# A fused attention and GLU kernel: first batch's loads re-paced, the chain of replicated rows moved, stores two blocks behind

## The chip, the cores and the metric

The kernel runs on one core of a Trainium2 chip. The metric is the device time of one execution in microseconds (us). Every time of a kernel below is a median of several executions, unless it is called a single run; every reading of a profile comes from one profiled execution of that kernel. The profile of the kernel before that the prediction read is of a run of 715.1 us, longer than all its timed runs at that time and marked as slow; a second profile of it, of an ordinary run, was taken among the experiments, and the trace kept with that run is of a third, shorter execution. The accounts below give all three, since they differ.

In the timed sets the runs marked slow are those over 1.5% above the fastest of their kernel in the set; the ratios below leave them out, the medians and ranges contain them.

## The reference

Two stages run one after the other. The input x has 4 batches of 12416 tokens with 128 channels.

```python
def mab(q, kv):
    s = scale * (q @ kv.transpose(0, 2, 1))
    a = np.exp(s - s.max(-1, keepdims=True))
    a /= a.sum(-1, keepdims=True) + 1e-09
    return a @ kv
h = mab(I, x)            # 32 inducing points attend to the tokens
y = mab(x, h)            # the tokens attend to the 32 results
gate = 1 / (1 + np.exp(-(y @ w_gate)))      # w_gate, w_val: 128 x 1536
out = (gate * (y @ w_val)) @ w_out          # w_out: 1536 x 128
```

## The kernel before

A block is 512 tokens; a batch has 24 blocks. For every block TensorE, ScalarE and VectorE work as a pipeline: TensorE makes six pairs of gate chunks `g` and twelve value chunks (`va` two at a time, `vb` one), ScalarE takes tanh of each `g` into `T`, and VectorE makes `u = (T + 1) * v`, one instruction for each `va` or `vb`, whereupon TensorE adds up the output `acc`. VectorE needs about 7 us for a block (666.2 us of busy time over 97 blocks in the profile below). In six blocks of 24 (3, 7, 11, 15, 19, 23: the "shared" blocks) three of the twelve value chunks are multiplied by GpSimd instead.

A string, PLAN, fixes the interleaving of these steps. Everything else is hung into that order: `at(n, k, f)` emits `f` at step `k` (0 to 3) of block `n` (a shared block is short: what stands at its step 0 is emitted with step 1), `put` queues a job for TensorE. Each engine and each queue is given its work in exactly the order emitted. Two side chains matter here.

The chain of replicated rows makes, for every 4096 tokens, the normalised weights that the GLU blocks read (`rep`). Eight blocks use one `rep`. `n` is a block about six before the first use:

```python
def rep_events(n, b, d):
    put(n, 1, "s2", b, d)              # TensorE scores, ScalarE exp
    at(n + 1, 0, e2_dma, b, d)         # transpose e2 -> e2n       (sync queue)
    at(n + 1, 3, s2_sum, b, d)         # row sums rs, a tree of 5  (GpSimd)
    at(n + 2, 3, s2_rec, b, d)         # rc = 1 / rs               (VectorE)
    at(n + 2, 3, a2_mul, b, d, 0)      # a = e2n * rc              (GpSimd)
    at(n + 2, 3, a2_mul, b, d, 1)
    at(n + 3, 0, a2_dma, b, d, 0)      # transpose a -> a2T        (sync queue)
    at(n + 3, 1, a2_dma, b, d, 1)
    at(n + 3, 2, rep_put, b, d, 0)     # a2T -> DRAM tile dt       (sync queue)
    at(n + 3, 3, rep_put, b, d, 1)
    at(n + 4, 0, rep_get, b, d, 0)     # dt -> rep, 4 copies       (sync queue)
    at(n + 4, 1, rep_get, b, d, 1)
```

The chain of the next batch loads x in six quarters of 512 KB (`xq`, issued on GpSimd's queue), transposes each (`xT`, sync queue) and computes the scores `s_1` and sums `h` for it between the GLU steps. Finished output blocks are transposed (`on`, sync queue) and stored (GpSimd's queue), one block after they are done:

```python
loads = ((1, 0), (2, 0), (5, 0), (6, 0), (8, 0), (9, 0))     # first batch
at(n0 + ln + 1, 2, xT_dma, nb, q)
# ... (cut)
if stores and (done_out[n] == 10 or n >= NBK - 2):
    stores.popleft()()
```

The softmax here doesn't subtract the row's maximum and nothing guards it: scores larger than these inputs give would overflow.

## Time and profile before

| | before |
|---|---|
| median (3 runs) | 709.57 us (707.03 to 714.02) |
| profiled run (slow) | 715.09 us |
| profiled span | 713.3 us |
| VectorE busy | 666.2 us |
| VectorE idle, 40 to 700 us | 20.2 us |

The head of the page of the kernel before: busy time by engine, then the span in 40 slices of 17.8 us, a digit for each (9 is 90% busy or more; PEclk is the clock granted to TensorE, in tenths).

```profile
span 713.3 us, 13070 instructions
PE 679.8 (95%) x4561; PEld 238.2 (33%) x4561; DVE 666.2 (93%) x792; ACT 662.5 (93%) x773; POOL 309.6 (43%) x389
...
DVE  2599686999999999999999999999999999999997
PEclk9999898999999999999999999999999999999999
```

VectorE, ScalarE and TensorE are all near full except at the start and in slices 5 to 7. So idle time of VectorE is the account to keep. Its longest waits in the steady part are these (engine, tile and line, what it waited for; total us, times, longest):

```profile
DVE u_8_1670 L495 <- PE vb_2_1668 L428: 6.4, 1, 6.4
DVE u_4_1402 L495 <- PE va_1_1399 L428: 4.2, 1, 4.2
```

TensorE's own waits name the cause, the first for scores on quarters 2 and 3, the second for rep:

```profile
PE s_1_1657 L767 <- DMA xT_154<-xq_2_1174: 4.2, 1, 4.2
PE g_0_1394 L428 <- DMA rep_1_1278<-dt_1_0_1230: 3.6, 2, 2.4
```

With the slow clock after each gap (0.50 from 85 to 90 us, 0.52 from 110 to 115), the first (80 to 95 us, rep_1) cost 6.4 us of VectorE's time and the second (104 to 121 us, xT of quarter 3) 7.8 us. The transfers between 60 and 130 us (last number: us from issue to landing):

```profile
xq_2_1174<-in_x_dram POOLq DMA_DIRECT2D x1, 512.0 KB, 8.6
xq_3_1283<-in_x_dram POOLq DMA_DIRECT2D x1, 512.0 KB, 10.8
...
a2T_1_0_1172<-a_0_1_0_1147 SPq DMA_TRANSPOSE x1, 4.0
a2T_1_1_1204<-a_0_1_1_1149 SPq DMA_TRANSPOSE x1, 8.0
```

The same a2T transpose of 128 KB takes 4.0 or 8.0 us. The second, issued at 72.2 us, had two 512 KB loads beside it, issued at 67.3 and 68.4; the first, issued at 66.4, met them only towards its end.

These are a reciprocal of the row sums on VectorE and, below it, the sums on GpSimd, in the kernel before (start, duration, engine, line, operation):

```profile
188.49 0.68 DVE L495 SCALAR_TENSOR_TENSOR u_8_2828<-T_4_2773,vb_2_2826 128x512 f16<-128x512 f16 x1
189.09 0.35 DVE L361 RECIPROCAL rc_0_2835<-rs_0_2734 128x32 f32<-128x32 f32 x1
```

```profile
182.20 1.26 POOL L511 TENSOR_TENSOR x_2_2626<-vt_2_2627,v_19_1_2624 128x512 f16<-128x512 f32 x1
...
185.41 1.14 POOL L353 TENSOR_TENSOR tree_1_0_2735<-e2n_0_2682 128x512 f32<-128x512 f16 x1 [1.40 <-DMA e2n_0_2682<-e_1_0_2679]
...
188.33 0.24 POOL L353 TENSOR_TENSOR rs_0_2734<-tree_1_0_2741 128x32 f32<-128x32 f32 x1
```

The sums come after the last product `x` of the shared block, end at 188.57, and the reciprocal starts at 189.09 with nothing to wait for. It has 0.5 us to spare. (These lines do not depend on the slow run's gaps; the ordinary run's eleven reciprocals wait 1.2 us in all.)

### The profile page before, as it was taken

To read this page: it belongs to the slowest core of one execution; us is meant where nothing else is said; L and a number is where in the kernel's file an instruction comes from. 1 tells how busy PE (TensorE), PEld (TensorE's weight loads), DVE (VectorE), ACT (ScalarE), POOL (GpSimd) and SP (SyncE) were. 2 spreads that over 40 slices of the span, in tenths; PEclk is the share of its full clock that TensorE was granted. 3 is DMA by queue.
4 is the path that set the end of the run, shared out by engine and by line. 5 is a ranking of instruction groups with operands and counts; after the bars stand their busy time and mean duration, and the time that the engine had idled before them with its cause. 6 is when DMAs were issued, how large, how long until landed. Compare 5 with 4: busy or idle time off the path is not lost.

```text
span 713.3 us, 13070 instructions
## 1 busy us (share of the span) xinstructions
PE 679.8 (95%) x4561; PEld 238.2 (33%) x4561; DVE 666.2 (93%) x792; ACT 662.5 (93%) x773; POOL 309.6 (43%) x389
## 2 busy tenths in 40 slices
PE   7899788999999999999999999999999999999997
PEld 4433222333333323333333333333333333333334
DVE  2599686999999999999999999999999999999997
ACT  4699776999999999999999999999999999999995
POOL 5234504452643541743541651634723534633423
PEclk9999898999999999999999999999999999999999
DMA  9599999884888792397688584454192353263222
GB/s 177 95 110 158 183 71 187 139 184 84 145 188 130 125 209 60 90 183 135 106 187 148 111 164 103 94 142 77 39 169 67 60 149 80 60 150 74 60 53 75
DMA packets 163955, 85.95 MB, mean 120 GB/s; under 512 B 133392, under 2 KB 148144, under 8 KB 163888
## 3 DMA queue, kind: packets, MB, share of 16 engines
q1 hardware_dynamic: 143904, 45.95, 38.2%
q0 software_dynamic: 19696, 39.03, 27.1%
q8 instruction: 35, 0.57, 0.4%
q14 instruction: 32, 0.26, 0.2%
q10 hardware_dynamic: 288, 0.13, 0.1%
HBM read 39.34 MB, written 28.31 MB: 95 GB/s over the span
## 4 chain that ended last, share of the span: by engine, by line
PE 64%; ACT 10%; DVE 9%; DMA 8%; issue 4%; POOL 3%; SPq 1%; DVEq 0%; ACTq 0%; POOLq 0%
DMA xq_4_132<-in_x_dram 2%; DMA xT_154<-xq_3_1283 2%; DMA a2T_1_1_1204<-a_0_1_1_1149 1%; SPq L397 1%; DMA a1n_2_3819<-e_2_2_3703 1%; DMA on_7763<-oT_7761 1%; DMA a1n_2_6256<-e_3_2_6162 1%; DMA on_5277<-oT_5275 1%; PE acc_1687 L538 1%; DMA rep_1_1278<-dt_1_0_1230 0%; PE acc_4267 L538 0%; PE acc_2641 L538 0%; PE acc_1770 L538 0%; PE acc_5765 L538 0%; PE acc_3334 L538 0%
## 5 line engine op out<-in xcount | busy, mean ns | idle before, releaser
L538 PEld LDWEIGHTS <-wo_117 128*128 128x128 f16 x1152 | 94.2, 98 | 147.7 <-issue 93.8
L428 PEld LDWEIGHTS <-hw_165 32*128 32x128 f16 x466 | 19.1, 91 | 59.9 <-issue 54.5
L428 PEld LDWEIGHTS <-hw_168 32*128 32x128 f16 x456 | 19.8, 91 | 56.2 <-issue 53.9
L428 PEld LDWEIGHTS <-hw_167 32*128 32x128 f16 x464 | 19.4, 91 | 54.1 <-issue 51.2
L428 PEld LDWEIGHTS <-hw_166 32*128 32x128 f16 x468 | 19.4, 91 | 52.4 <-issue 49.8
L428 PEld LDWEIGHTS <-hwp_172 128*128 128x128 f16 x120 | 11.7, 97 | 14.3 <-issue 4.7
L428 PEld LDWEIGHTS <-hwp_169 128*128 128x128 f16 x110 | 10.7, 98 | 15.8 <-issue 8.6
L428 PEld LDWEIGHTS <-hwp_171 128*128 128x128 f16 x112 | 10.9, 97 | 13.7 <-issue 5.8
L428 PEld LDWEIGHTS <-hwp_170 128*128 128x128 f16 x108 | 10.5, 97 | 14.6 <-issue 7.3
L566 POOL DMA_DIRECT2D out_dram<-on_1411 x1 | 0.5, 532 | 21.3 <-DMA on_1411<-oT_1409 21.3
L245 PEld LDWEIGHTS <-ones 128*128 128x128 f16 x96 | 6.9, 97 | 8.1 <-DMA a1n_2_6256<-e_3_2_6162 2.1
L190 PE MATMUL warm<-ones 128*128 128x512 f16 x16 | 5.6, 530 | 1.5 <-DVE ones L140 1.5
L767 PE MATMUL s_1_1657<-xT_154,indT 128*32 128x512 f16 x8 | 1.2, 605 | 5.8 <-DMA xT_154<-xq_2_1174 4.2
L495 DVE SCALAR_TENSOR_TENSOR u_8_1670<-T_4_1559,vb_2_1668 128x512 f16<-128x512 f16 x1 | 0.7, 690 | 6.4 <-PE vb_2_1668 L428 6.4
L214 ACT ACTIVATE e_1_2_1666<-s_1_1657 128x1024 f16<-128x1024 f32 x1 | 1.0, 1024 | 5.9 <-PE s_1_1657 L767 5.9
L310 POOL COPY hwp_169<-hw_165 32x128 f16<-32x128 f16 x2 | 0.6, 282 | 12.9 <-ACT hw_165 L303 12.8
L239 ACT ACTIVATE a1nt_205<-s1t_203 128x32 f16<-128x32 f32 x1 | 0.2, 198 | 6.0 <-PE s1t_203 L235 6.0
L495 DVE SCALAR_TENSOR_TENSOR u_4_1402<-T_2_1358,va_1_1399 128x1024 f16<-128x1024 f16 x1 | 1.2, 1222 | 4.2 <-PE va_1_1399 L428 4.2
L566 POOL DMA_DIRECT2D out_dram<-on_888 x1 | 0.5, 537 | 10.5 <-DMA on_888<-oT_886 10.5
L508 POOL TENSOR_TENSOR vt_0_6656<-v_59_2_6653,T_0_6643 128x512 f32<-128x512 f32 x1 | 1.1, 1150 | 8.3 <-PE s_2_6670 L324 8.3
L551 ACT ACTIVATE o_10374<-acc_10278 128x256 f32<-128x256 f32 x2 | 0.8, 384 | 4.3 <-PE acc_10278 L528 3.8
L482 ACT ACTIVATE T_0_1397<-g_0_1394 128x1024 f16<-128x1024 f32 x1 | 1.0, 1024 | 3.9 <-PE va_1_1399 L428 3.9
(4281 smaller groups left out, 2802.5 us busy)
## 6 DMA issues: line engine op xcount, KB each, us to landing
xq_0_120<-in_x_dram POOLq DMA_DIRECT2D x1, 512.0 KB, 5.1
xq_1_122<-in_x_dram POOLq DMA_DIRECT2D x1, 512.0 KB, 6.9
xq_2_128<-in_x_dram POOLq DMA_DIRECT2D x1, 512.0 KB, 8.3
xq_3_130<-in_x_dram POOLq DMA_DIRECT2D x1, 512.0 KB, 10.2
xq_4_132<-in_x_dram POOLq DMA_DIRECT2D x1, 512.0 KB, 13.4
xq_5_134<-in_x_dram POOLq DMA_DIRECT2D x2, 256.0 KB, 14.1
xq_0_770<-in_x_dram POOLq DMA_DIRECT2D x1, 512.0 KB, 6.2
xq_1_875<-in_x_dram POOLq DMA_DIRECT2D x1, 512.0 KB, 10.1
```

Source lines behind the costliest of these rows:

```text
L190: nc.tensor.matmul(ps[:, 0:TOK], ones[:, 0:P], ones[:], start=True, stop=True)
L214: nc.scalar.activation(out=e1[:, 0:w], in_=ps[:, 0:w], func=AF.Exp, scale=SCALE)
L245: nc.tensor.matmul(ps[:, cs:cs + P], ones[:, 0:P], a1n[(b, q)][:, j, :], start=first and j == 0, stop=last and j == 3,)
L397: nc.sync.dma_start(rep[g * M:(g + 1) * M, 4 * i:4 * i + 4].rearrange("m r j t -> m r (j t)"), dt[:].rearrange("(r m) t -> m r t", m=M),)
L428: nc.tensor.matmul(ps[:, ds(col, TOK)], weights(k["b"]), rep[rows, 4 * k["i"] + k["r"]], start=True, stop=True,)
L482: nc.scalar.activation(out=Ts[(bi, p)][:, :, 0:T], in_=ps[:].rearrange("p (a t) -> p a t", a=2)[:, :, 0:T], func=AF.Tanh, scale=0.5,)
L495: nc.vector.scalar_tensor_tensor(out=u[:, :, 0:T], in0=Ts[(bi, j0 // 2)][:, j0 % 2:j0 % 2 + n, 0:T], scalar=1.0, in1=ps[:].rearrange("p (a ...
L508: nc.gpsimd.tensor_tensor(out=t[:], in0=v, in1=Ts[(bi, j0 // 2)][:, j0 % 2 + jj, :], op=ALU.mult)
L538: nc.tensor.matmul(accs[bi][:, 0:T], wo16[:, j, :], u, start=(c == 0), stop=(c == NJ - 1))
L551: nc.scalar.activation(out=o32[:, h:h + w, :].rearrange("p b c -> p (b c)"), in_=accs[bi][:, ds(h * P, w * P)], func=AF.Copy, scale=0.5,)
L566: nc.gpsimd.dma_start(out[ds(row0, QT)].rearrange("(p j) c -> p j c", j=QT // P)[:, 4 * k["r"]:4 * k["r"] + 4, :], on[:],)
L767: nc.tensor.matmul(ps[r * M:(r + 1) * M, ts(i, TOK)], indT[:], xTs[a[0]][:, ds(q * QT + r * TOK, TOK)], start=True, stop=True,)
```

## The change

The intent is to remove the two early gaps: the loads of the first batch come one at a time, the big transposes stand apart from the fetches of rep, these are half a block later, and stores wait another half block, so that GpSimd isn't held by an output transpose (21.3 us at one in the profile read). With this, row sums and reciprocal move one step earlier inside their blocks, and most chains also move one block earlier (`rep_events` at 1 and 9 instead of 2 and 10, and `fin` at 15 instead of 16 in the first batch).

```diff
     def rep_events(n, b, d):
         put(n, 1, "s2", b, d)
         at(n + 1, 0, e2_dma, b, d)
-        at(n + 1, 3, s2_sum, b, d)
-        at(n + 2, 3, s2_rec, b, d)
-        at(n + 2, 3, a2_mul, b, d, 0)
-        at(n + 2, 3, a2_mul, b, d, 1)
-        at(n + 3, 0, a2_dma, b, d, 0)
-        ... (cut)
+        at(n + 1, 2, s2_sum, b, d)
+        at(n + 2, 2, s2_rec, b, d)
+        for i in range(2):
+            at(n + 2, 2, a2_mul, b, d, i)
+            at(n + 3, 0, a2_dma, b, d, i)
+            at(n + 3, 3, rep_put, b, d, i)
+            at(n + 4, 2, rep_get, b, d, i)
... (cut)
-        rep_events(n0 + 2, b, 1)
-        rep_events(n0 + 10, b, 2)
+        rep_events(n0 + (2 if b == 0 else 1), b, 1)
+        rep_events(n0 + 9, b, 2)
... (cut)
-                loads = ((1, 0), (2, 0), (5, 0), (6, 0), (8, 0), (9, 0))
-                s1s, s1t, fin = (5, 9, 12), 6, 16
+                loads = ((0, 3), (2, 2), (4, 1), (6, 0), (7, 3), (9, 2))
+                s1s, s1t, fin = ((5, 1), (9, 0), (12, 1)), 6, 15
+                wait = 4                        # 6 in the later batches
... (cut)
-                at(n0 + ln + 1, 2, xT_dma, nb, q)
+                at(n0 + ln + (lk + wait) // 4, (lk + wait) % 4, xT_dma, nb, q)
... (cut)
-        if stores and (done_out[n] == 10 or n >= NBK - 2):
+        while stores and (n >= NBK - 2 or len(stores) > 1 and done_out[n] == 4):
```

The string PLAN is replaced too (the interleaving of 97 blocks), and the h jobs move a little.

More of the change, by code (lines that the diff above doesn't have):

```diff
@@ L26 @@
     "GAGBWGAabGBcGAfeGBdGAhBWgJ AGilkjBGGAabcBGAfGBedGAhGgBiG AlkjBGGAbacBGAfWBedGAhJBgG "
-    "AilkjBGGAabcBGAfWBedGAhGgBiG AlkjBGGAbaBcWAGfeBGdAGBhGg AGilkBjGAJBabcAGefBGdAGhgBGi "
-    "AGlBkjJAGBaGbAGcGBefGAdhGBgG AikljBGGAbBaefGAdGBchG AgGBikGAljBJAGaBGbcGAGfBedG "
-    "AhGgBiGAlJBkGAjJBGAGbacBfeG AGdhBgiAGlkjBGGAbBJaAGcfBGe AGdhBGgAGiBkljGAGBabef "
-    "AGdBJcGAhgBGikAGljJBGAGbaBcfG AGedBGgAGhBilGAGkjBJAGBaGbcG AefGBdGAhgGBiGAkljBJAGbaGBcf "
-    "AGeGdBhGAgiWBlGAkjJBG AGabfBecGAGdBghGAikGBlJjAGBaGbcG AfGBedGAhJBgGAilkjBGGAabBcefG "
@@ L32 @@
-    "AdGBghGAilkjBGGAbaBGcGAfBJe AGdhBGgAGilBkjGAGBabef AGdcBGgGAhiBkljGAGBbacfAGedgGBhG "
-    "AilkjBGGAbacBWAGfBedGAhGgBiG AlkjBGGAbacBJAGfBGeAGdghBG AGilBkjGAGBbafeAGdcGBG "
-    "AghBGiAGklBJjAGGBbacfAGedBGg AGhiBGkAGljBJAGBGabcGAeGfBdG AgGhBiGAlGkBjGAJbaBcAGfeBGdh "
-    "AGgiGBkGAljBJAGbGBGa AGBefdGAGchBgGAiGBlkjGAGBabce AGfBJdAGhgBWiAGkBljGAGBbacf "
-    "AGedGBghAGilkjBGGAabBGcAGefBGd AGhgBGiAGlkjBJGABbGafG AedGBcGAhgBWiGAklBjJGAaGbBcG "
-    "AfeGBdGAhJBgGAilkjBGGAbacBfe AGdgGBhGAilkjBGGAaBJbAGceBGf AGdhBGgAGilkBjGAGBabef "
@@ L38 @@
-    "AGdcGBgGAhiBGkAGljBJAGBGbaceG AGfBdghGAiWBklGAjJBGAGabcBfG AGedBhGAgGBGAGilkJjBGAaGbBGcf "
-    "AGedBWhAGgilBkjGAJaBbG AceGBfGAdhBWgGAilBkjGAJbBaG AcfGBeGAdBWghAGilkBjGGAabBceG "
-    "AfGdBgGAhiBGGAlkjBGGAbacGBe AGfdBhGAGgilBkjAGGBbafe AGcdBGhAGgiBlkjGAGBabceAGfdBgG "
-    "AGhikBljGAGBabcGAefBGdAGhgBGi AGlBkjGAGaBbcGAJBfeGAdGBhgG AilkjBGGAabfBedGAcGBhgG "
-    "AikljBJGAbGBacGAfWBedAGhgGBiG AlkGBGAjBJAGbBGacGAfGBedG AhGgBiGAlGkBjGAGBbacfAGeBJd "
-    "AGghBGiAGlkjBJGABbaGfG AedBchGGAgiBkljGAGBabceGAfBdGgh AGikljBGAJBbaGAcWBfeGAdGhBgG "
@@ L44 @@
-    "AilkjBGAGabBcGAeGBGAGfdBGh AGgikBGAGlBjJAGBbGae AGfdBGhGAgciBGAGlkBjJGABbGacG "
-    "AfGeBdGAhgWBiGAkljBJAGbacBfG AeGBdGAhJBgGAilkjBGGAbacBfGG AedBghiGAlkjBGGAbaBfedG "
-    "AGhBgciAGlkBjJGAaBbGcfAGedWBhgG AiGlBkGAjJBGAGabBcWAGfBedG AGhgBiGAlGkBjJAGBbaGGcAGfBJe "
-    "AGdBGhgGAilkBjGAGbBafeG AdcGBgGAhiGBkGAljBJGAbacBfG AeGBdhGAgGiBlGAkjBWGAabBcefG "
-    "AdGBghGAilkjBGGAbacBfeGAGBdGh AGgilBkjGAGBefbaAGdgBWh AGicBkljGAGBbacGAefdBGAGghBiG "
-    "AGlkjBGAGBbacGAfeBWdAGhgBGi AGlBkjGAGBabcGAefGBdGAhGBgiG AkljBGGAfeBbadGAhWBgcG "
@@ L50 @@
-    "AilkBjGGAabBcGAfeGBdGAhgBGiG AlkBjGGAbaBcAGfWBedGAhgGBiG AlkjBJAGbacBGAfGeBGAdWBhgG "
-    "AikljBGGAfedBabGAGhBgiG AclkjBGGAabcBGAGfBedGAhWgBiG AGlkBjGAGBbacAGefBWAGdhgBG "
-    "AGiBlkjGAGBabcAGefBdJAGGhBgG AikGlBjGAGBabfeAGdgBWh AGciBkljGAGBabcGAefBGdAGhgiBG "
-    "AGkljBGAGBbacGAfeBWdGAhgBGi AGlBkjGAGBabcGAefGBdGAJBhgG AilkjBGGAfeBbadGAGhgBcG "
-    "AilBkjGGAabBcGAfBGedGAhgWiBG AlkjBGGAbacBGAGfeBdGAGBhgiG AlkjBGGAabcBGAGfeBdGAGBGhg "
-    "AGiBlkjGAGBefabAGdhBWgG AicBlkjGAGBbacGAefBGdAGhgBGi AGlkBjGAGBbacGAefBWdGAhgBGi "
@@ L56 @@
-    "AGlBkjGAGBbacGAefGBdGAhGgBiG AlkjBGGAfebBadGAgWBhcG AikBljGGAabBcGAfeGBdGAhGBgiG "
-    "AlkBjGGAbBacAGfBWedAGhgBGiG AlkBjGAGbaBcGAefBGdGAhGgBiG AlkjBGGAbafBeGAdWBhgG "
-    "AcikBljGABaGbAcfeBdAhgBilkj"
+    "AilkjBGGAabcBGAfWBedGAhGgBiG AlkjBGGAbaBcWfAGeBGdAGhBgG AGilBkjAGJBbaAGcfBGeAGdgBGh "
+    "AGiBGlAGkBJjAGGBabceAGfdBGgG AhiBGkAGljBJAGbGBaJ AGcBGefGAdgWBhGAilkjBGGAbacBeG "
+    "AfJBdGAghWBiGAlkjBJAGabcBfeG AdGhBgGAilkjBGGAabBcGGAefBdJ AGhBGgiGAlkGBjJAGBGbafG "
+    "AedBGcGAhBJgGAiklBjGAGaBbcf AGedGBgGAhikBljGAGBbacfAGedBGhG AgiBGlAGkjBJGABbGaGAGceBJ "
@@ new lines @@
+    "AGBfGdgGAhiGBlJkjAGBGabfG AedBGcGAgBJhAGilkjBGGAbBacfG AeGdBhGAgJBiGAlkjBWGAabcBfG "
+    "AGedBhGAgGiBlGAkGjBGAGBabcf AGedBGhgGAikljBGGAbaBfeG AGdgBhGAiGBlkGAjcBWGAabcBfG "
+    "AGeBdhGAgGiBlGAkjBGGAabBceG AGfdBgGAJBhiGAlGkBjGAGBabcf AGedBGhgAGilkjBGGAabfBeG "
+    "AdGBchGAgGiBlGAkJBjGGAbacBeG AfGdBhGAgJBiGAlkjBJGAaBGbcG AeGfBdGAhgGBiGAlGkBjAGGBbacfG "
+    "AedhBgGGAilkjBJGABGbafG AedGBhGAgiGBkGAljBcWGAaBbcfG AeGdBgGAhJBiGAlkjBWGAabcBefG "
+    "AGdhBgGAilkjBGGAabBcfeGAGdBGhg AGiBkljGGAfBebaGAdgWBhG AicGBkGAljJBGAGabBcJAGfGBedG "
@@ new lines @@
+    "AhBJgAGilkBjGAJbBaGAcfWBeG AdhGBgGAikljBGAGabcBeGAfdGBGhg AGilkjBGGAfeBdGbAGahBWg "
+    "AGiklBGAGjBcJAGBGabcGAfeGBdG AhgiBGGAklBjJGABbWacGAfeGBdG AhgGBiAGlkJjBGAbGaGBcGAfGeBdG "
+    "AhGgBiGAlkjBWGAbafBJ AGBeGcAGdBhgGAGiBlkjAGJbBa AGcfBGeAGdBgGhAGilkBjGAGBabcf "
+    "AGedBGhAGgBGikAGljBGGAabBGc AGeBfGdAGhgBWAGilBkjG AGBbaefAGdhgBGAGickBljGAGBabce "
+    "AGfdBGhAGgikBljGAGBabceAGfdGBg AGhiBGlAGkBjJAGaBbcGAGfeBdG AhGgBiGAlkjBGGAbaeBfdG "
+    "AGchBgGAilkjBJGAaGBbcGAfeGBdG AhgBGiGAlBJkAGjBJAGBGbacG AfGBedGAhgGBiGAkljBGGAbaBGc "
@@ new lines @@
+    "AGfeBdhgGAGilkjBJAGBWabf AGedGBgGAhiGBlGAkjcBWAGabBceG AfdGBgGAhJBiGAlkBjWGAabBcfG "
+    "AeGdBhGAgGiBlGAkGBjGAGBabcf AGedBGhgAGilkjBGGAbaeBfG AdGhBgGAcGBilGAkjBJAGabGcBJG "
+    "ABJefGAdgGhBiGAlkjBWGAabcBJ AGfeBdGAGhBgGAiGBlkjAGGBbacG AfGeBdGAhgGBilGAkjBWG "
+    "AfebBadGAGhBgikGAljcBJGAbBWacG AfeGBdGAghBGiGAlkjBJAGbBGacG AfeGBdGAhgiBGJlkjAGBbacGGAfBJe "
+    "AGdgGBhGAilBkjGAGbaBefG AdcGBgGAhiGBlGAkjBJGAbBacfG AeGdBgGAhGBikGAljBGGAabBceG "
+    "AfGdBGAhGBgiGAlGkBjGAGBabcG AefGBdGAhGBgiGAlkBjWG AfeaBbdGAhgGBiGAlkjcBGGAbacBfG "
@@ new lines @@
+    "AeGBdgGAhGiBlGAkjBWGAbaBceG AGfBdgGAhiGBlGAkGBjGAGBabcf AGedBGhAGgikBljGAGBbaef "
+    "AGdhGBgAGciBGkAGljBWAGBabcf AGeBGdgGAhiGBlGAkjBJAGabBceG AfGdBgGAhiGBlGAkjBGGAabBcfG "
+    "AGeBdghGAilGkBjGAGBefb AGadBGgAGhiBGAGlkBjcGAGBabce AGfdhBGAGgiBlkjGAGBabcfAGedGBh "
+    "AGgiBGkAGlBJjAGGBbacAGeBfGd AGhgBGikGAljBGGAbaeBfG AdGcBhGAgGiBlGAkjBWGAbaBceG "
+    "AGfBdgGAJBhiGAlkjBWAGabcBfG AGBedhGAgGiBGAlGBkjGAGBabcf AGedBGhgGAikljBGGAbafBedG "
+    "AGgBhiGAklBjcAGGaBbcfGAedGBgG AhilBkjGAGBbacAGfeBWdAGhgBGi AGlBkjGAGBabcGAefGBdGAhgGBiG "
@@ L59 @@
+    "AlkjBGGAfeBbadGAgWBhiG AckBljGGAbBacGAfeGBdGAhgGBiG AlkBjGGAbaBcGAfWBedGAhgBGiG "
+    "AlkjBGAGbBacGAeGBfdGAGhBgi AGlkjBGGAbaBfedAGhWBgiG AclBkjGGAabBcGAfeGBdGAhgBGiG "
+    "AlkjBGGAbBacGAfWBedGAhgiBGG AlkjBGAGBbacGAefBGdGAhGBgiG AlkjBGGAfeBbaGAdWBhgG "
+    "AicBlkjGAGBabcAfedBAghBilkj"
 )
@@ L693, in rep_events @@
         at(n + 1, 0, e2_dma, b, d)
-        at(n + 1, 3, s2_sum, b, d)
-        at(n + 2, 3, s2_rec, b, d)
-        at(n + 2, 3, a2_mul, b, d, 0)
-        at(n + 2, 3, a2_mul, b, d, 1)
-        at(n + 3, 0, a2_dma, b, d, 0)
-        at(n + 3, 1, a2_dma, b, d, 1)
-        at(n + 3, 2, rep_put, b, d, 0)
-        at(n + 3, 3, rep_put, b, d, 1)
-        at(n + 4, 0, rep_get, b, d, 0)
-        at(n + 4, 1, rep_get, b, d, 1)
+        at(n + 1, 2, s2_sum, b, d)
[5 more added lines that the diff above has]
+            at(n + 4, 2, rep_get, b, d, i)
     def m_mul():
@@ L734 @@
             if b == 0:
-                loads = ((1, 0), (2, 0), (5, 0), (6, 0), (8, 0), (9, 0))
-                s1s, s1t, fin = (5, 9, 12), 6, 16
-                hs = ((8, 1), (9, 1), (12, 2), (13, 1), (14, 3), (15, 1))
+                loads = ((0, 3), (2, 2), (4, 1), (6, 0), (7, 3), (9, 2))
+                s1s, s1t, fin = ((5, 1), (9, 0), (12, 1)), 6, 15
+                hs = ((7, 1), (7, 3), (11, 1), (11, 3), (14, 1), (14, 3))
+                wait = 4
             else:
                 loads = ((-10, 0), (-7, 0), (-4, 0), (-1, 0), (2, 0), (5, 0))
-                s1s, s1t, fin = (-2, 5, 9), 0, 14
-                hs = ((1, 1), (3, 1), (7, 1), (8, 1), (12, 1), (13, 1))
+                s1s, s1t, fin = ((-2, 1), (5, 1), (9, 1)), 0, 14
+                hs = ((1, 1), (3, 1), (8, 1), (8, 3), (12, 1), (13, 1))
+                wait = 6
             for q, ((ln, lk), (hn, hk)) in enumerate(zip(loads, hs)):
                 at(n0 + ln, lk, load_x, nb, q)
-                at(n0 + ln + 1, 2, xT_dma, nb, q)
+                at(n0 + ln + (lk + wait) // 4, (lk + wait) % 4, xT_dma, nb, q)
                 put(n0 + hn, hk, "h", nb, q)
             at(n0 + loads[1][0], 1, load_tail, nb)
-            at(n0 + loads[1][0] + 1, 3, xTt_dma, nb)
-            for e, sn in enumerate(s1s):
-                put(n0 + sn, 1, "s1", nb, [2 * e, 2 * e + 1])
-                at(n0 + sn + 1, 1, a1_dma, nb, [2 * e, 2 * e + 1])
+            at(n0 + loads[1][0] + 2, 1, xTt_dma, nb)
+            for e, (sn, sk) in enumerate(s1s):
+                put(n0 + sn, sk, "s1", nb, [2 * e, 2 * e + 1])
+                at(n0 + sn + 1, 0, a1_dma, nb, [2 * e, 2 * e + 1])
             put(n0 + s1t, 1, "s1t", nb)
```

## The prediction

> **What bounds the kernel now.** In the busy time by stretch, VectorE is busy 639.8 of the 660 us between 40 and 700 us, TensorE 638.6, ScalarE 632.7: a three-engine pipeline with little to take away. What can be gained are VectorE's 20.2 us of idle time there:
>
> - 80 to 95 us: 6.4 us. The timeline shows block 8's g_0 reach TensorE at 80.6 and wait for the replicated rows rep_1 until 84.7. Their a2T_1_1 transpose took 8.0 us from 72.2, beside two 512 KB loads issued at 67.3 and 68.4.
> - 104 to 121 us: 7.8 us. The score job s_1 waits to 110.6 for the transpose xT of quarter 3, issued at 97.4, after 5.8 us of issuing quarter 2's and 4.2 us for an output transpose.
> - near 265, 365, 425 and 533 us: about 4 us. The chain of waits shows two waits for a1n transposes, and two where GpSimd waits on an output transpose before a store and delivers products late.
>
> After the first two stalls the granted clock is 0.5 for about 5 us. [...] (0.50 at 85 to 90 us), and the 1.5 us stalls leave it at 1.00.
>
> **What the change does.** Only order moves. The first batch's loads stand apart instead of in pairs; both a2T transposes follow each other at the start of block 5; stores come half a block (3.5 us) later, so GpSimd should not sit 21.3 us on one output transpose (at 88 us) with a load behind it.
>
> **Stall 2 should nearly vanish.** Quarter 3's transpose is now ahead of two output transposes, at about 84 us instead of 97, needed at about 97: 6.5 us of 7.8. **The late small ones** lose 3 of 4 us: output transposes get 3.5 us more before a store waits, and the h jobs stand further from their a1n.
>
> **Stall 1 mostly stays.** Quarter 2's transpose now stands between the a2T transposes and the dt copies. Nothing on GpSimd holds quarter 3's load back: it goes out near 67 us, not at its nominal 74, and collides with that transpose, which then takes 8 us or more, not the 4.3 us of an undisturbed one. The sync queue then issues block 5's output transpose (ready about 77) before the rep fetches; with 3.6 us to land, rep_1 arrives at 82 to 86, while g_0 of block 8 wants it at 80.6. I expect 4.5 us lost instead of 6.4.
>
> **Sum.** 6.5 + 3 + 2 = 11.5 us less in the profiled run (713.3 us, a long one). The median run's stalls must be smaller, so I take about 11 off 709.6: **698.5 us**, range 691 to 706 (removing all 20 us would give about 691). Chances: faster by over 2% 0.35, within 2% 0.61, slower 0.04.
>
> **What would show it.** VectorE idle between 104 and 121 us under 2 us, no wait of s_1 for xT; g_0 of block 8 waits 1.5 to 5 us for rep_1 near 80 us[...]; no GpSimd wait over 10 us at a store; VectorE busy still about 666 us.
>
> **What would make it wrong.** If quarter 2's transpose is quick, both stalls go: 692 to 694. If it is slow, stall 1 grows. The new interleaving could cost tenths per block, which I could not see.

## The result

The changed kernel takes 749.2 us (median of 4 runs, 748.77 to 750.69) against 708.38 for the kernel before (4 runs). The ratio is 1.056 (95% interval 1.050 to 1.063). Ratios are the mean time of one kernel's fast runs over that of the other's in the same rounds, so not quite the ratio of the medians.

The head of the page of the changed kernel, to be set against that of the kernel before:

```profile
span 747.0 us, 13067 instructions
PE 691.9 (93%) x4561; PEld 237.8 (32%) x4561; DVE 668.0 (89%) x792; ACT 664.1 (89%) x773; POOL 308.2 (41%) x389
...
DVE  2699478899799799999999799799999799899997
PEclk9999889999899999999999999899999999999999
```

VectorE is as busy as before (668.0 us against 666.2), but there are dips all along the span: besides slices 5 to 8 at 11, 14, 23, 29, 32 and 35. The kernel before has no such row of dips. Its waits (same columns as before):

```profile
DVE u_4_1402 L495 <- PE va_1_1399 L428: 12.8, 1, 12.8
DVE rc_2_1867 L361 <- POOL rs_2_1771 L353: 4.0, 1, 4.0
...
DVE rc_2_6774 L361 <- POOL rs_2_6688 L353: 3.4, 1, 3.4
DVE rc_1_5940 L361 <- POOL rs_1_5858 L353: 3.2, 1, 3.2
DVE rc_1_8323 L361 <- POOL rs_1_8242 L353: 3.1, 1, 3.1
DVE rc_1_3505 L361 <- POOL rs_1_3418 L353: 3.0, 1, 3.0
DVE rc_0_2716 L361 <- POOL rs_0_2628 L353: 3.0, 1, 3.0
DVE rc_2_9082 L361 <- POOL rs_2_8995 L353: 3.0, 1, 3.0
```

There are two kinds. One is the wait near 80 us, now 12.8 us. The other is new: seven times the reciprocal `rc` waits 3 to 4 us for GpSimd's row sums `rs`, 22.7 us in all (an eighth, in the first batch, waits 1.3 us; three of the eleven do not wait). The surroundings of one of them, on VectorE and then on GpSimd, for the same chain as those shown of the kernel before:

```profile
187.53 0.68 DVE L495 SCALAR_TENSOR_TENSOR u_3_2702<-T_1_2626,vb_1_2700 128x512 f16<-128x512 f16 x1
191.18 0.35 DVE L361 RECIPROCAL rc_0_2716<-rs_0_2628 128x32 f32<-128x32 f32 x1 [2.96 <-POOL rs_0_2628 L353]
191.44 1.16 DVE L495 SCALAR_TENSOR_TENSOR u_6_2725<-T_3_2675,va_2_2722 128x1024 f16<-128x1024 f16 x1
```

```profile
182.95 1.15 POOL L508 TENSOR_TENSOR vt_0_2611<-v_19_2_2608,T_0_2597 128x512 f32<-128x512 f32 x1 [7.91 <-ACT v_19_2_2608 L832]
...
187.98 1.15 POOL L353 TENSOR_TENSOR tree_1_0_2629<-e2n_0_2575 128x512 f32<-128x512 f16 x1
...
190.90 0.24 POOL L353 TENSOR_TENSOR rs_0_2628<-tree_1_0_2635 128x32 f32<-128x32 f32 x1
```

The reciprocal now starts when the sums end. Ahead of the sums stand the two products of the shared block, from 182.95 to 188.0. And u_6, which stands behind the reciprocal, has its value chunk from matmuls that TensorE began at 187.84 (va_2 in its timeline, 0.39 us each) and its T from ScalarE by 186.6, but it began only at 191.44: it wasn't waiting for its data but for its turn. TensorE ran dry in the meantime. Its busy time in single microseconds (stretch, length, busy us and matmuls, granted clock, DMA share, GB/s):

```profile
189.00:190.00 1.00, 0.95 (x6) 1.00 0.00 0
190.00:191.00 1.00, 0.00 (x0) 1.00 0.04 8
...
192.00:193.00 1.00, 0.34 (x2) 0.50 0.02 3
...
```

The clock stays at 0.50 until 198 us. So this wait of 2.96 us was followed by some six at half clock; around the other six waits the clock stood at 0.50 too, for two to six whole microseconds, and the 22.7 us of waiting became 32.5 us of idle VectorE. By stretches, from the busy times in four profiles (the kernel before in the slow run that the prediction read, in an ordinary run of 709.6 us and in a third execution with a span of 704.9 us, both told under the experiments):

| VectorE idle, us | before, slow run | before, ordinary run | before, third | after |
|---|---|---|---|---|
| start, 0 to 40 | 22.0 | 23.3 | 22.5 | 22.8 |
| first early gap: 40 to 95, after to 98 | 6.8 | 1.0 | 5.8 | 14.6 |
| second early gap: from there to 121, after to 127 | 7.8 | 0.8 | 0.7 | 1.6 |
| around the seven reciprocals | 0 | 0 | 0 | 32.5 |
| the rest, to 700, after to 740 | 5.7 | 11.7 | 4.8 | 2.7 |
| end | 4.9 | 4.9 | 4.9 | 4.9 |
| all | 47.1 | 41.6 | 38.7 | 79.0 |

Against the ordinary run the sum differs by 37.4 us; with 1.7 us more of busy time that is the 39.2 us between the spans of 747.0 and 707.8 us. The reciprocals took 32.5 us, the first early gap 13.6, and 9.0 came back in the rest. Against the third profile the first gap is worth 8.8 and the rest 2.1. The share of the reciprocals is the same against all three. The sync queue of the changed kernel (start, us to issue):

```profile
69.98 1.28 SPq L384 DMA_TRANSPOSE a2T_1_1_1176<-a_0_1_1_1130  x1
...
72.71 11.25 SPq L193 DMA_TRANSPOSE xT_154<-xq_2_1103  x1
84.05 0.53 SPq L390 DMA_DIRECT2D dt_1_0_1252<-a2T_1_0_1174  x1
...
88.03 2.78 SPq L397 DMA_DIRECT2D rep_1_1337<-dt_1_0_1252  x4
```

and the transfers from 60 to 100 us:

```profile
xq_3_1278<-in_x_dram POOLq DMA_DIRECT2D x1, 512.0 KB, 13.6
...
a2T_1_0_1174<-a_0_1_0_1128 SPq DMA_TRANSPOSE x1, 10.2
a2T_1_1_1176<-a_0_1_1_1130 SPq DMA_TRANSPOSE x1, 13.9
...
xT_154<-xq_2_1103 SPq DMA_TRANSPOSE x1, 13.4
```

Here issuing quarter 2's transpose held the sync queue from 72.7 to 84.0; the first copy behind it went out at 84.05. But the a2T transposes ahead of it were slow as well, 10.2 and 13.9 us against 4.0 and 8.0, with the load of quarter 3 in flight from 70.2 for 13.6 us, and that of quarter 2, issued at 66.5, until 72.7.

### The profile page after: what moved, and what is told of

Same layout as the page of the kernel before. It is cut to its first block, busy times and chain, and to the rows that moved or that the text cites. A ratio compares the mean times of both kernels' runs of the same rounds, so it can differ in the third digit from the quotient of the medians.

```text
span 747.0 us, 13067 instructions
## 1 busy us (share of the span) xinstructions
PE 691.9 (93%) x4561; PEld 237.8 (32%) x4561; DVE 668.0 (89%) x792; ACT 664.1 (89%) x773; POOL 308.2 (41%) x389
## 4 chain that ended last, share of the span: by engine, by line
PE 64%; ACT 9%; POOL 8%; DVE 8%; issue 4%; DMA 4%; SPq 2%; DVEq 0%; ACTq 0%; POOLq 0%
DMA xq_4_132<-in_x_dram 2%; SPq L193 2%; DMA rep_1_1337<-dt_1_0_1252 1%; DMA xq_2_1103<-in_x_dram 1%; PE acc_2754 L538 1%; DMA e2n_1_974<-e_0_1_962 0%; PE acc_6837 L538 0%; PE acc_6010 L538 0%; PE acc_8370 L538 0%; PE acc_7441 L538 0%; PE acc_8742 L538 0%; PE acc_2366 L538 0%; PE acc_3663 L538 0%; PE acc_7727 L538 0%; PE acc_3230 L538 0%
## 5 line engine op out<-in xcount | busy, mean ns | idle before, releaser
L428 PEld LDWEIGHTS <-hw_168 32*128 32x128 f16 x464 | 19.4, 91 | 63.5 <-issue 61.0
L428 PEld LDWEIGHTS <-hwp_169 128*128 128x128 f16 x114 | 11.3, 100 | 16.6 <-issue 9.0
L495 DVE SCALAR_TENSOR_TENSOR u_4_1402<-T_2_1354,va_1_1399 128x1024 f16<-128x1024 f16 x1 | 1.2, 1222 | 12.8 <-PE va_1_1399 L428 12.8
L428 PE MATMUL g_0_1393<-rep_1_1337,hw_165 32*128 32x512 f16 x2 | 1.2, 590 | 12.0 <-DMA rep_1_1337<-dt_1_0_1252 11.9
L508 POOL TENSOR_TENSOR vt_0_10061<-v_95_2_10058,T_0_10048 128x512 f32<-128x512 f32 x1 | 1.1, 1149 | 12.7 <-ACT v_95_2_10058 L832 12.7
L508 POOL TENSOR_TENSOR vt_0_9714<-v_91_2_9711,T_0_9701 128x512 f32<-128x512 f32 x1 | 1.2, 1151 | 12.6 <-ACT v_91_2_9711 L832 12.6
L310 POOL COPY hwp_169<-hw_165 32x128 f16<-32x128 f16 x2 | 0.6, 282 | 13.4 <-ACT hw_165 L303 13.3
L508 POOL TENSOR_TENSOR vt_0_6682<-v_59_2_6679,T_0_6668 128x512 f32<-128x512 f32 x1 | 1.1, 1148 | 11.1 <-PE vb_2_6709 L428 11.1
L508 POOL TENSOR_TENSOR vt_0_9367<-v_87_2_9364,T_0_9354 128x512 f32<-128x512 f32 x1 | 1.2, 1151 | 11.0 <-ACT v_87_2_9364 L832 11.0
L508 POOL TENSOR_TENSOR vt_0_7107<-v_63_2_7104,T_0_7087 128x512 f32<-128x512 f32 x1 | 1.1, 1150 | 10.4 <-ACT v_63_2_7104 L832 10.4
L508 POOL TENSOR_TENSOR vt_0_3832<-v_31_2_3829,T_0_3807 128x512 f32<-128x512 f32 x1 | 1.2, 1152 | 9.6 <-ACT v_31_2_3829 L832 9.6
## 6 DMA issues: line engine op xcount, KB each, us to landing
xq_4_132<-in_x_dram POOLq DMA_DIRECT2D x1, 512.0 KB, 14.3
xq_5_134<-in_x_dram POOLq DMA_DIRECT2D x2, 256.0 KB, 14.7
xq_1_922<-in_x_dram POOLq DMA_DIRECT2D x1, 512.0 KB, 12.8
```

The lines of the kernel that those rows point to most:

```text
L310: nc.gpsimd.tensor_copy(out=pads[b][rows, 2 * i + jj, :], in_=hws[b][rows, p, :])
L428: nc.tensor.matmul(ps[:, ds(col, TOK)], weights(k["b"]), rep[rows, 4 * k["i"] + k["r"]], start=True, stop=True,)
L495: nc.vector.scalar_tensor_tensor(out=u[:, :, 0:T], in0=Ts[(bi, j0 // 2)][:, j0 % 2:j0 % 2 + n, 0:T], scalar=1.0, in1=ps[:].rearrange("p (a ...
L508: nc.gpsimd.tensor_tensor(out=t[:], in0=v, in1=Ts[(bi, j0 // 2)][:, j0 % 2 + jj, :], op=ALU.mult)
```

## The experiments

Theory A: the seven waits come from the place of the reciprocal on VectorE, too soon after sums that queue behind products on GpSimd. Rival A2: the new interleaving stalls anyway. Theory B: rep_1 is late because of the big transpose ahead of it on the sync queue. Rival B2: rep_1 is late because the load of quarter 3, which nothing holds back on GpSimd, collides with the transposes. All kernels gave correct results. The kernel before ran beside each set; its medians there were 707.8 to 708.5 us over the timed sets. Profiles of the experiments list tiles without their numbers.

### The kernel before once more

Unchanged, for an ordinary profile.

> The kernel before once more, unchanged, for a profile of an ordinary run: the profile at hand is of a run of 715 us, 1% above the median. Expected: span 704 to 709 us, no wait of a reciprocal for row sums (longest under 0.5 us), and the two early gaps somewhat smaller than 6.4 and 7.8 us of VectorE's idle time, 8 to 12 us together.

709.6 us, at the median; a single run, so its state is marked unknown. VectorE by stretches (length, busy us and instructions, granted clock, DMA share, GB/s):

```profile
80.00:95.00 15.00, 14.38 (x18) 1.00 1.28 208
104.00:121.00 17.00, 16.81 (x19) 1.00 1.14 176
240.00:260.00 20.00, 15.51 (x19) 0.86 0.85 178
420.00:440.00 20.00, 15.93 (x20) 0.83 0.43 91
```

The early gaps are gone in this run (0.6 and 0.2 us); the expectation of 8 to 12 us was wrong. Instead there are two late gaps of 4.5 and 4.1 us with a fallen clock. TensorE's waits name them:

```profile
PE h L245 <- DMA a1n<-e: 4.0, 2, 2.4
```

These are the `h` jobs that wait for their a1n transposes, 1.6 and 1.5 us in the slow run. The trace that was kept with this run is of yet another execution of the same kernel (span 704.9 us). There the first early gap is back, since rep_1 is 3.7 us late, and the other three stretches lose 0.7, 1.4 and 1.3 us:

```profile
80.00:95.00 15.00, 9.62 (x11) 0.89 1.07 184
```

So this kernel has several narrow places, and the run decides which of them opens; one more profile doesn't give a typical one. The change moved the h jobs of quarters 2 and 3 away from their a1n, and in its profile they do not wait; no run here undid that part alone.

### The reciprocal two steps later

```diff
-        at(n + 2, 2, s2_rec, b, d)
+        at(n + 3, 0, s2_rec, b, d)
         for i in range(2):
-            at(n + 2, 2, a2_mul, b, d, i)
+            at(n + 3, 0, a2_mul, b, d, i)
```

> The changed kernel with the reciprocal of the row sums and the two multiplications moved two steps later (from step 2 of the block to the start of the next one), nothing else. Theory A (VectorE stands still at seven reciprocals because GpSimd's row sums come 3 to 4 us after them): the seven waits of the reciprocal for rs (23.7 us in sum) go, and with them about 30 us of VectorE's idle time: about 719 us. Rival A2 (the new interleaving of GLU steps itself is what stalls, and the reciprocal only happens to stand there): the gaps stay in other instructions, time stays above 740. The wait for rep_1 near 80 us should stay at about 12 us in both.

712.4 us (704.40 to 715.28), ratio 1.000 to the kernel before (0.991 to 1.009). Two of the four runs (715.0 and 715.3) are marked slow; the fast two, 704.4 and 709.9, have a mean of 707.1. No reciprocal waits any more. A2 falls: the same interleaving runs without these stalls. (The expectation's sum of 23.7 us should have been 22.7.) The gain, 37 us by the medians and 42 by the fast runs, is more than the 32.5 us at the reciprocals, and the expectation that the first gap would stay failed: in the profiled run, the fastest of four, rep_1 was only 2.3 us late.

The traces suggest why. GpSimd multiplies with the reciprocal between issuing the loads of quarters 2 and 3. Here it waited 3.2 us for the later reciprocal, so the loads went out at 63.5 and 70.4 us; in the changed kernel it was 66.5 and 70.2. With 6.8 us between them instead of 3.7, a2T took 6.2 us (median of two) instead of 10.2 and 13.9. The run with this repair and quarter 2's transpose moved shows the same (6.2 us apart, a2T 5.9), the run with half the repair does not (4.1 us apart, a2T 10.1). So the repair of the reciprocals also parts two loads. No run changed their distance alone.

### One step later: the dose

The same two lines, at `(n + 2, 3)`.

> The changed kernel with the reciprocal and multiplications one step later, half of the first repair: a dose test. Under theory A each of the seven waits of about 3.3 us shrinks by what VectorE does in one step, 1.9 us, to about 1.4 us: VectorE loses about 10 us at them instead of 32, time about 725 us; if a wait only has to be on the wrong side of a threshold, it is either 749 or 714.

724.7 us (721.89 to 726.22).
VectorE's reciprocals wait 8.0 us in all, seven times, longest 1.7: 1.1 us on average instead of 3.2, and the time lies between. VectorE's idle time after 98 us is 20.4 us, where the changed kernel has 41.7 and the full repair 9.2: 11 of the 32.5 us remain, where about 10 were expected. The first gap is smaller too (8.5 us from 40 to 98 instead of 14.6), so not all of the gain is the dose. A wait shrinks by about the 1.9 us of VectorE's work in one step (a `va` and a `vb`: 1.22 + 0.68 us).

### The sums ahead of the products

```diff
-        at(n + 1, 2, s2_sum, b, d)
+        at(n + 1, 1, s2_sum, b, d)
```

> The changed kernel with GpSimd's row sums one step earlier, so that they stand ahead of the shared block's products on GpSimd; the reciprocal stays where it is on VectorE. Theory A in its full form (the sums are late because they queue behind about 5 us of products): the reciprocal waits fall from 3 to 4 us to under 1 us each, time about 719 us. If instead the e2n transposes land late and the products are not to blame, the waits stay at 3 us or more. A part of the gain may be lost where products come later.

718.0 us (710.41 to 724.60, the last marked slow), ratio 1.012. One reciprocal still waits, 1.4 us. So the delay of the sums was the queue behind the products, not the e2n transposes. TensorE now waits 4.4 us in all for GpSimd's products, as they come later, and in this run it waited 11.3 us for rep_1.

### The chains one block later, as they were

```diff
-        rep_events(n0 + (2 if b == 0 else 1), b, 1)
-        rep_events(n0 + 9, b, 2)
+        rep_events(n0 + 2, b, 1)
+        rep_events(n0 + 10, b, 2)
```

> The changed kernel with the chains of replicated rows put back where the kernel before had them, one block later (at 2 and 10 of a batch, not 1 and 9), nothing else; the steps inside the block stay new. Six of the seven late reciprocals then stand in a block whose products do not go to GpSimd, behind sums that no product delays; the seventh (first chain of batch 1) is not moved. Theory A: six waits go, one of about 3 us stays, time 720 to 726 us. If the step inside the block is what counts (2 instead of 3), all seven stay and the time is above 742.

716.7 us (712.01 to 721.70), ratio 1.011.

Only 4.0 us of waits of reciprocals are left, in three. The largest, 3.0 us, is that of the chain which wasn't moved (VectorE loses 2.9 us between 180 and 200 us). The time is a little better than expected, and the first gap stays as it was (14.4 us). So it is less the step inside the block than the block: at 1 and 9, the row sums are emitted in blocks 2 and 10 of a batch, where the products of shared blocks 3 and 11 are emitted too, and the reciprocal in the short blocks 3 and 11 that follow.

The changed kernel holds a control of its own, in the chain at 9 of batch 1. It has the same place, but there PLAN sends the first product of the shared block to GpSimd only behind the sums, which end at 301.8 us. Its reciprocal doesn't wait (GpSimd, then VectorE):

```profile
302.92 1.15 POOL L508 TENSOR_TENSOR vt_0_4265<-v_35_2_4262,T_0_4242 128x512 f32<-128x512 f32 x1 [1.12 <-ACT v_35_2_4262 L832]
```

```profile
307.12 0.34 DVE L361 RECIPROCAL rc_2_4344<-rs_2_4244 128x32 f32<-128x32 f32 x1
```

The first chains of batches 2 and 3 moved by the step alone, stay out of the shared blocks, and don't wait either. The reciprocal that waits 1.3 us, in the first chain of all, is outside too; its sums waited for the e2n transpose, not for products.

### Quarter 2's transpose behind the fetches

```diff
-                at(n0 + ln + (lk + wait) // 4, (lk + wait) % 4, xT_dma, nb, q)
+                xk = 4 * ln + lk + wait + (5 if b == 0 and q == 2 else 0)
+                at(n0 + xk // 4, xk % 4, xT_dma, nb, q)
```

> The changed kernel with quarter 2's transpose of the first batch moved behind the fetches of the replicated rows on the sync queue, nothing else. Theory B (the 512 KB transpose ahead of the copies blocks the sync queue for 11 us): the wait of block 8's g_0 for rep_1 falls from 11.9 us to 4 us or less, time 738 to 743. Rival B2 (the loads that GpSimd sends early collide with the small a2T transposes, which then land 10 to 14 us after issue whatever stands behind them): the a2T landing times stay at 10 us or more and the wait stays at 8 us or more. The seven reciprocal waits stay in both.

743.4 us (741.32 to 744.19). The wait for rep_1 fell from 11.9 to 3.8 us, as theory B wanted; but the a2T transposes still took 10.5 us (median of two), as B2 wanted. B had its wait right (4 us or less) and B2 its a2T (10 us or more), but B2's wait (8 us or more) failed. So both causes seem to act.

### The load of quarter 3 behind the first products

```diff
-                loads = ((0, 3), (2, 2), (4, 1), (6, 0), (7, 3), (9, 2))
+                loads = ((0, 3), (2, 2), (4, 1), (6, 1), (7, 3), (9, 2))
```

(The transpose of that quarter is kept at its place.)

> The changed kernel with the load of quarter 3 of the next batch held behind the first products on GpSimd (it then goes out near 83 us, not at 70), its transpose where it was. Rival B2 (collision of that load with the transposes): a2T lands in under 6 us instead of 10 to 14, the sync queue issues quarter 2's transpose in under 5 us instead of 11.2, and the wait for rep_1 falls from 11.9 us to under 5 us. Theory B (order on the sync queue alone): a2T and the issue time stay, the wait stays at 9 us or more.

734.9 us (732.88 to 736.39), 14 us better than the changed kernel. What is left of the wait for rep_1 in TensorE's list:

```profile
PE g L428 <- DMA rep<-dt: 0.7, 1, 0.7
```

The load went out at 82.3 us. Issuing quarter 2's transpose took 3.9 us instead of 11.3, and a2T 7.1 us (median of two; expected was under 6). VectorE lost 1.6 us from 40 to 98 us instead of 14.6. So the collision was the larger cause: with it gone, the transpose ahead of the copies did no harm.

### Both repairs

The later reciprocal and the later load together.

> Both repairs in the changed kernel: the reciprocal and multiplications two steps later, and the load of quarter 3 behind the first products. If the two causes are separate and add up, the time is 749 less about 35 less about 14, so 698 to 702 us, with neither a reciprocal wait nor a wait for rep_1 over 1 us; that would be about 1% better than the kernel before. If they overlap, or a new stall opens, 705 us or more.

701.7 us (700.65 to 702.70, 5 runs), ratio 0.9915 to the kernel before (0.988 to 0.995): this version beats both kernels, the kernel before by under 2%. Its page:

```profile
span 699.5 us, 13067 instructions
...
DVE  2599999999999999999999999999999999999997
PEclk9999999999999999999999999999999999999999
```

VectorE loses 6.0 us between 40 and 694 us, where the ordinary run of the kernel before loses 13.4 between 40 and 700; that difference of 7.4 us fits the 6.7 us between the medians (the third profile loses 11.3). No clock loss is left in the steady part (mean granted clock 1.00 over the span).

The gain of 47.5 us is less than the sum of the two alone (36.8 and 14.3), as the first repair also took most of the first gap. By stretches the two causes stand apart (VectorE idle, us, from the busy times):

| | 40 to 98 | 98 to the end |
|---|---|---|
| changed kernel | 14.6 | 41.7 |
| later reciprocal | 4.4 | 9.2 |
| later load | 1.6 | 40.8 |
| chains one block later | 14.4 | 14.7 |
| both repairs | 1.8 | 9.1 |

After 98 us the later reciprocal is worth 32.5 us, with or without the later load, and the load next to nothing there.

### The repaired kernel with the old stores

```diff
-        while stores and (n >= NBK - 2 or len(stores) > 1 and done_out[n] == 4):
+        if stores and (done_out[n] == 10 or n >= NBK - 2):
```

> The repaired kernel (both repairs) with the stores as they were in the kernel before, one block behind. If the later stores are worth something, the waits of TensorE or GpSimd on output transposes come back (two of about 1 us in the kernel before) and the time is 2 to 4 us above the repaired one; if GpSimd's waits at stores cost nothing here, the two are within 0.3%.

710.6 us (709.94 to 712.54), ratio 1.005: the later stores are worth 9 us here, far more than expected. GpSimd in that run, near the largest gap (VectorE lost 5.2 us from 240 to 260 us):

```profile
249.71 0.53 POOL L566 DMA_DIRECT2D out_dram<-on  x1 [8.91 <-ACT T L482]
250.26 1.17 POOL L508 TENSOR_TENSOR vt<-v,T 128x512 f32<-128x512 f32 x1
```

The store holds GpSimd for 8.9 us with the products of a shared block behind it, and TensorE then waits 3.3 us for them. (The view names ScalarE's T for this wait; for the store before it, which waited 6.33 us, it names an output transpose. That a transpose was the cause here too is the author's estimate.)

### The kernel before with the new stores alone

The same edit, the other way round, in the kernel before.

> The kernel before with the new rule for stores (two blocks behind) alone. In the repaired kernel this rule was worth 9 us. Here the 21.3 us wait of GpSimd at a store near 88 us, with the load of quarter 4 behind it, and the two late waits of about 1 us at products should go: 702 to 706 us. If the rule only pays together with the new interleaving, 708 or more. The first stall (rep_1 late, 6.4 us) should stay in both cases.

709.3 us (706.77 to 722.90, the last marked slow), ratio 1.003 (0.998 to 1.007): nothing. The rule paid only with the new interleaving. The first stall, which was expected to stay, is absent from the profiled run (VectorE loses 1.2 us from 40 to 98 us). In the profiled run (span 705.9 us) TensorE waited five times for products, 3.3 us in all. Each interleaving seems to be fitted to one place of the stores; that it was made so is a guess.

### Two combinations that were worse than the repair

The later reciprocal with quarter 2's transpose behind the fetches:

> The changed kernel with the later reciprocal and with quarter 2's transpose behind the fetches of the replicated rows (the load of quarter 3 stays early). In the run with that transpose moved alone, rep_1 was still 3.8 us late; so about 3 us slower than the repair that holds the load back: 702 to 707 us, with a wait for rep_1 of 1 to 4 us.

713.3 us (709.02 to 716.17), not the 702 to 707 expected. rep_1 was only 1.3 us late, but the scores `s_1` waited 9.4 us for xT, since the sync queue needed 22.8 us to issue quarters 2 and 3 one after the other. The wait only moved from the first gap to the second.

The earlier sums with the later load:

> The other repair of the reciprocals (row sums ahead of the products on GpSimd) together with the later load of quarter 3. The later load was worth 14 us in the changed kernel with its 12 us wait for rep_1; with earlier sums the products come later, which cost 4.4 us of TensorE waits when tried alone. So 704 to 710 us, slower than the repair by a later reciprocal (701.7).

708.0 us (707.13 to 708.60): as expected. TensorE waited 3.6 us for products and VectorE 2.5 us at two reciprocals.

## Why the prediction was wrong

It said 698.5 us, with 4% for slower by over 2%; the kernel takes 749.2.

- **"Only order moves. ... The new interleaving could cost tenths per block, which I could not see."** This is the step that failed: the sum had no term for a wait that the new order makes, beyond "tenths per block". It looked for the cost of the new order in the GLU steps and not in the one instruction of the side chain that stands in VectorE's queue. The cost was there to be read without a run: in the built kernel's order GpSimd has two products of 2.5 us and a sum of 3.2 us in a row ahead of the reciprocal, and the kernel before had 0.5 us to spare. It was worth 32.5 us in the profile. The prediction's list of what moves had the stores, loads and a2T, but not the reciprocal, which in seven of eleven chains moves into a shared block, behind sums that stand behind its products.
- **"What can be gained are VectorE's 20.2 us of idle time there."** That was right for the slow run; the ordinary one had 13.4 us and the third 11.3. The places were not the kernel's but the run's: the two early gaps of 14.2 us, on which 8.5 of the 11.5 us of expected gain rested, cost 0.8 us in the ordinary run and 6.1 in the third, nearly all of it in the first gap. One profile of a long run was taken for the kernel.
- **"Stall 1 mostly stays ... 4.5 us lost instead of 6.4."** The mechanism was right as far as it went: the load went out at 70.2 (predicted: 67), collided with quarter 2's transpose, and that held the sync queue. The size was off: the transpose took 13.4 us ("8 us or more"), rep_1 landed near 95 (predicted 82 to 86), g_0 waited 11.9 us (predicted 1.5 to 5). VectorE lost 14.6 us from 40 to 98 us, where the kernel before lost 6.8 in the slow run, 1.0 in the ordinary one and 5.8 in the third to 95. What the prediction left out is that the a2T transposes ahead were slowed too (10.2 and 13.9 us): with quarter 2's transpose moved away, rep_1 was still 3.8 us late. The sentence "If it is slow, stall 1 grows" named this, but the range did not hold it.
- **"Stall 2 should nearly vanish."** Right for the changed kernel: no wait of s_1 for xT, and 1.6 us lost. But the ordinary run before had lost only 0.8, and the third 0.7.
- **"The late small ones lose 3 of 4 us."** Right against the slow run that it read: outside the named gaps the steady part lost 2.7 us instead of 5.7 (11.7 in the ordinary run, 4.8 in the third). But of the four places that it named, those near 365 and 533 had cost VectorE nothing in that run (12.00 of 12 us and 14.00 of 14 us busy). Not shown one by one is which edit did it; the comparison of store rules shows that the later stores matter with the new interleaving.
- **"No GpSimd wait over 10 us at a store."** Nearly: two of 10.5 and 10.7 us remain, instead of 21.3 and 10.5.
- **"VectorE busy still about 666 us."** Right: 668.0.
- **The clock.** The prediction had a fallen clock after the two long gaps only. The seven gaps at the reciprocals (TensorE waited 2.6 to 3.7 us for u) came with a clock of 0.50 too: mean granted clock 0.969 over the span, 0.986 and 0.996 in the ordinary and the third run before.

The floor of about 691 us in the prediction could not be tested. With both repairs the kernel reaches 701.7 us, and VectorE's idle time outside start and end is then 6.0 us.

What stays open: how much the new PLAN is worth by itself, since no kernel here has it without the moved events; what the moved h jobs are worth by themselves; what the distance of the two loads is worth by itself; and why the gaps of one kernel lie at different places in different runs.

## What to carry to other kernels

An instruction of a side chain that stands in the queue of the busiest engine must come late enough for its slowest producer: here u_6, with its data ready, began only behind a reciprocal that waited 2.96 us, and a reciprocal of 0.35 us cost 32.5 us in seven places. When such an event moves by a step or a block, look up what stands ahead of its producer in the producer's own order, there and not on average. Pacing by program position was no pacing on GpSimd, which ran ahead (quarter 3's load, nominally at 74 us, went out at 70.2): put a transfer behind an instruction that really ends late, as the later load did (82.3 us). And profile more than one run before deciding which gap to close.

## What the runs show of transposes and the clock

- A 128 KB transpose took 2.4 us apart from the loads (an output transpose at 62.7 us in the kernel before; the median of all 96 output transposes in the run with the old stores is 2.5) and 10.2 to 13.9 us beside two 512 KB loads from another queue (the two a2T in the changed kernel).
- With transposes and loads in flight, issuing one 512 KB transpose took 11.25 us of the sync queue (13.4 us to landing), and two took 22.8 us in the run with the later reciprocal and quarter 2's transpose moved. Those that landed in 4.3 or 4.4 us took 1.3 to 2.0 us to issue (61.1, 110.1 and 122.7 us in the changed kernel, 58.9 in the kernel before). The dt copy behind the long one went out at 84.05 us, when its issue had ended.
- In the changed kernel a TensorE gap of 2.7 us (189.95 to 192.66) came with a clock of 0.50 from 192 to 198 us; in the kernel before, the waits of 1.5 and 1.6 us for a1n (to 264.1 and 429.8 us) left it at 1.00. In the run with half the repair TensorE waited for u 16 times, 1.7 us at the longest: the clock was 0.88 and 0.95 from 120 to 140 us (a mean for each 10 us), 0.83 from 460 to 470, and 1.00 in the other 57 such stretches from 100 to 700 us. Which length of gap is enough was not shown.
- The waits in VectorE's queue came with a fallen TensorE clock: 22.7 us of waits cost 32.5 us.
